# Cross terms of the second feed-forward product as seven block products in five of eight groups

## The chip, the cores and the metric

The kernel runs on one core of one Trainium2 chip. The metric is the device time of one execution in microseconds, as the median of several runs. Engines are named as the profile names them: PE is TensorE's matrix multiply, PEld its weight load, DVE is VectorE, ACT is ScalarE, POOL is GpSimd, SP is the engine that issues the DMAs.

## The reference, cut to what matters

x has 2048 tokens of D = 448 elements, F is 1792. One branch is a spectral filter over the whole array, the other a mixer whose last step is the feed-forward part that the change touches:

```python
xn = layernorm(x)
# spectral branch
A = irfft2(rfft2(xn) * (w_r + 1j * w_i), s=(S, D))
# mixer branch
h  = gelu(layernorm(xn) @ w1)
hs = concat(shift(h, +1, -1, +2, -2 on the four quarters)) @ w2
x1 = xn + hs
h2 = gelu(layernorm(x1) @ w3) @ w4
out = x + A + x1 + h2
```

The whole is computed close to float32 although TensorE is fed 16-bit numbers.

## The kernel before

**Halves.** Every float32 operand of a product is split into a high and a low float16 half, and a product is three: high by high, high by low and low by high. The last two are the cross terms.

**Tiles.** The 2048 tokens are 16 blocks of 128; block b holds tokens b, b + 16 and so on. The feed-forward part runs over eight groups G of two blocks (256 tokens) and, in each, over seven passes fp, each of which takes two of the fourteen 128-row slices of F. `front(G, fp)` (line 745) makes the 256 x 256 hidden values transposed: 22 matmuls of 256 columns at line 427 into one PSUM bank, whose tag ("mm", "tr") the caller gives. ACT then applies the gelu in place (line 753) and scales and copies the high half to `h` (line 756), and DVE subtracts to get the low half (line 757). `back(G, fp)` (line 761) multiplies by w4: for each of the two blocks, two slices by three products, twelve matmuls of 448 columns at line 776, added up over the seven passes in two PSUM banks of tag "acc". For the last block the columns are cut in two halves of 224 in two banks, so group 7 has 18 matmuls a pass: six of 448 and twelve of 224. After pass 6 DVE scales the sum and adds it to the block's tile (line 788, or line 783 with the store for groups 6 and 7, whose blocks wait in `rest`).

**Order.** `mlp` (line 791) issues fronts ahead of backs: two ahead in groups 0 to 2, with fronts over the tags mm and tr (four banks), one ahead in groups 3 to 7, with mm alone (two banks). It is called for group 0, groups 1 and 2, groups 3 to 5, group 6 and group 7; a call does not run ahead into the next. The tile framework orders each engine's queue by a planner with priorities: evacuations (EVAC) come first, the feed-forward matmuls (FILL) come last and fill what the spectral branch leaves. `behind(key)` makes what follows not issue before an earlier instruction: the folds and step1 are spread over passes by FOLD and PACE, the inverse by `units`. Each engine then runs its queue in order.

**What runs beside it.** Before group 0: layernorms, w1, shifts, w2. In group 0, w4 is split into halves, two slices at a time (`w4_split`, line 841, ACT and DVE), hooked behind the fronts. In groups 0 to 2 the spectral branch folds x (`do_fold`, line 562: load of two blocks, ACT, then four adds on POOL), splits it (`step1_in`, lines 584 and 585) and multiplies (`step1`, line 594, bank tag "sp"). During groups 3 and 4 sixteen chunks go through `chunk_a`, `chunk_b`, `chunk_z`, `chunk_c` (pp in a "tr" bank, px and pu in "sp" banks). From group 4, pass 4, to the end of group 6 each pass carries one inverse block: DVE gathers U (line 709), `inv_a` multiplies (pe, line 717, bank tag "tr"), ACT copies (line 721), POOL adds and subtracts (lines 724 and 725), DVE does four more (lines 726 to 729), ACT and DVE split into vh (lines 731 and 732), and `inv_b` multiplies (py, line 739, bank tag "sp") and DVE adds it to the block (line 740). `finish` (line 554) adds the input again (line 551) and stores.

**Memory.** PSUM has four tags of two banks each: mm, tr, acc, sp. `x2mem` (line 222) holds first w4 as loaded, then the transposed layernorm output of all groups. `wsrc` feeds warm-up matmuls at the start.

## Time and profile before

| what | value |
|---|---|
| three runs | 413.22, 412.57, 413.07 us, median 413.07 |
| profiled execution, first to last instruction (span) | 409.9 us |
| granted TensorE clock, mean | 1.000 |
| busy DVE, ACT, POOL over the span | 294.8, 247.8, 116.8 us |
| instructions | 8512 |

The profile is one execution; it gives its span, and no time of its own beside that. The runs are some 3 us longer than the span, since they hold what lies before the first and behind the last instruction.

A group row gives the line, engine, operation, tiles written and read, shapes, the count, then the busy time in us, the mean of one in ns, and the idle time of the engine just before with what ended it. A matmul's duration overlaps the next one's, so 352 ns of a 448-column matmul is not what it costs: the chain of work in order of time shows the spacing.

### The profile page before, as it was taken

The numbers are of one execution on the slowest core, as the hardware profiler recorded it, in microseconds if no ns is written. First come the engines' busy times: TensorE is split into PE (matmuls) and PEld (weight loads), VectorE is DVE, ScalarE is ACT, GpSimd is POOL, SyncE is SP. The second block draws the span as 40 slices with busy tenths as digits, with TensorE's granted clock in tenths as the row PEclk, the third lists the DMA queues.
The fourth block names the chain that finished last, engine by engine and source line by source line (L and its number), as shares of the span: only waits on it lengthen the run. The fifth ranks groups of instructions, "written<-read, shape, count | busy, mean of one in ns | idle before, by whom it ended". The sixth has DMA issues, their size and how long they took to land.

```text
span 409.9 us, 8512 instructions
## 1 busy us (share of the span) xinstructions
PE 404.8 (99%) x3295; PEld 288.1 (70%) x3295; DVE 294.8 (72%) x642; ACT 247.8 (60%) x427; POOL 116.8 (29%) x206
## 2 busy tenths in 40 slices
PE   8999999999999999999999999999999999999996
PEld 4554556666677877776887887877776777677885
DVE  5989999898644658863689889875777787667122
ACT  4689994884738756861688888873343434342321
POOL 3889820002308745400021221111222221121000
PEclk9999999999999999999999999999999999999999
DMA  8999999907712283527056555610000213223001
GB/s 278 335 269 200 172 178 248 269 2 183 137 43 56 79 300 106 143 63 164 14 162 167 145 147 142 182 43 2 2 0 2 73 55 100 91 76 128 24 0 46
DMA packets 57208, 49.45 MB, mean 121 GB/s; under 512 B 41312, under 2 KB 52192, under 8 KB 57168
## 3 DMA queue, kind: packets, MB, share of 16 engines
q1 hardware_dynamic: 57168, 48.91, 45.5%
q8 instruction: 26, 0.43, 0.4%
q14 instruction: 14, 0.11, 0.1%
HBM read 35.06 MB, written 3.67 MB: 95 GB/s over the span
## 4 chain that ended last, share of the span: by engine, by line
PE 96%; DMA 1%; POOL 1%; DVE 1%; issue 0%; POOLq 0%
PE pw L427 33%; PE acc L776 31%; PE pw L501 9%; PE pw L456 6%; PE pu L697 3%; PE ps L594 3%; PE pp L651 2%; PE pe L717 2%; PE px L668 2%; PE py L739 2%; PE wps L812 2%; DMA h<-hs 1%; PE pta L406 1%; POOL w2s L273 0%; POOL w2s L901 0%
## 5 line engine op out<-in xcount | busy, mean ns | idle before, releaser
L427 PE MATMUL pw<-x2mem,w3p 128*128 128x256 f16 x1232 | 149.1, 272 | 0.0
L776 PE MATMUL acc<-w4p,hf 128*128 128x448 f16 (+1 forms) x714 | 138.0, 341 | 0.0
L427 PEld LDWEIGHTS <-w3p 128*128 128x128 f16 x1232 | 118.6, 98 | 19.0
L776 PEld LDWEIGHTS <-hf 128*128 128x128 f16 x714 | 69.4, 98 | 48.3 <-DVE hf L757 0.3
L753 ACT ACTIVATE pw<-pw,pe 128x512 f32<-128x512 f32 x56 | 36.7, 655 | 63.1 <-PE pw L427 62.0
L757 DVE SCALAR_TENSOR_TENSOR hf<-pw,h,hf 128x512 f16<-128x512 f32 x56 | 42.0, 749 | 44.7 <-ACT hf L756 44.3
L756 ACT ACTIVATE hf<-pw,h 128x512 f16<-128x512 f32 x56 | 38.3, 684 | 1.2
L501 PE MATMUL pw<-w2p,h 112*128 112x448 f16 x192 | 38.8, 352 | 0.1
L678 POOL TENSOR_TENSOR z<-te 128x450 f32<-128x450 f32 x16 | 16.0, 1001 | 72.9 <-DVE te L676 69.1
L456 PE MATMUL pw<-w1p,xT 128*128 128x448 f16 x176 | 34.9, 352 | 0.5 <-DVE h L875 0.5
L724 POOL TENSOR_TENSOR e<-e 128x226 f32<-128x226 f32 x16 | 11.5, 720 | 77.8 <-ACT e L721 74.6
L501 PEld LDWEIGHTS <-h 112*128 112x128 f16 x192 | 18.5, 98 | 16.9 <-DMA h<-hs 0.9
L456 PEld LDWEIGHTS <-xT 128*128 128x128 f16 x176 | 17.0, 98 | 16.4 <-ACT xT L416 0.7
L658 ACT ACTIVATE pf<-pp 64x450 f16<-64x450 f32 x32 | 17.3, 541 | 16.7 <-DVE pf L659 8.3
L721 ACT ACTIVATE e<-pe 128x452 f32<-128x452 f32 x16 | 8.8, 547 | 26.4 <-PE pe L717 26.4
L659 DVE TENSOR_TENSOR pf<-pp,pf 64x450 f16<-64x450 f32 x32 | 19.9, 621 | 5.8 <-ACT pf L658 5.6
L574 POOL TENSOR_TENSOR xr<-xf 128x452 f32<-128x452 f32 x8 | 8.9, 1109 | 35.9 <-issue 27.1
L673 ACT ACTIVATE te<-px 64x450 f32<-64x450 f32 x32 | 17.2, 537 | 0.5
L585 DVE TENSOR_TENSOR xh<-f,xh 128x452 f16<-128x452 f32 x16 | 13.4, 878 | 5.3 <-ACT xh L584 5.3
L732 DVE TENSOR_TENSOR vh<-e,vh 128x448 f16<-128x448 f32 x16 | 10.0, 624 | 9.7 <-ACT vh L731 9.7
L577 POOL TENSOR_TENSOR f<-xr 128x452 f32<-128x452 f32 x16 | 16.4, 1045 | 0.6
L726 DVE TENSOR_TENSOR e<-e 128x113 f32<-128x113 f32 x16 | 9.9, 619 | 7.8 <-POOL e L724 7.8
(171 smaller groups left out, 598.8 us busy)
## 6 DMA issues: line engine op xcount, KB each, us to landing
wc<-wf SPq DMA_DIRECT2D x32, 225.0 KB, 3.5
wl<-wf SPq DMA_DIRECT2D x8, 450.0 KB, 4.1
xf<-x SPq DMA_DIRECT2D x8, 448.0 KB, 3.5
xt<-x SPq DMA_DIRECT2D x3, 896.0 KB, 12.1
w3raw<-w SPq DMA_DIRECT2D x3, 896.0 KB, 15.3
xr<-x SPq DMA_DIRECT2D x12, 224.0 KB, 2.6
out<-xr SPq DMA_DIRECT2D x12, 224.0 KB, 2.0
gn<-c_g SPq DMA_DIRECT2D x16, 128.0 KB, 3.2
```

Of the source, the lines that this page charges most:

```text
L427: T.matmul(ps_out, wp[:, wi + t, cols], xT[:, xi + t, tok], start=t == 0 and wi + xi == 0, stop=t == 3 and wi == 4)
L456: m = T.matmul(pm[:, :D], xTs[g][:, xi + t, 128 * i:128 * i + 128], w1p[:, wi + t], start=t == 0 and p == 0, stop=t == 3 and p == 2)
L501: m = T.matmul(w2b[b][:, :D], hT[g][:112, 4 * hi + k, o:o + 128], w2p[:, wi, k], start=k == 2 and hi + wi == 0, stop=k == 3 and hi == 1)
L577: P.tensor_tensor(out=f[:, :, k:k + 2].rearrange("p b s d -> p s b d"), in0=u[:, :, 0], in1=u[:, :, 1], op=op)
L658: A.activation(out=hi, in_=src, func=AF.Copy)
L659: V.tensor_tensor(out=lo, in0=src, in1=hi, op=ALU.subtract)
L673: i = A.activation(out=e[64 * h:64 * h + 64], in_=px_[64 - 64 * h:128 - 64 * h, :2 * DF], func=AF.Copy)
L678: P.tensor_tensor(out=z, in0=t[:, 0], in1=t[:, 1], op=ALU.add)
L753: A.activation(out=pm, in_=pm, func=AF.Gelu_apprx_tanh, scale=r3)
L756: i = A.activation(out=h[:, 0], in_=pm, func=AF.Copy, scale=h3)
L757: j = V.scalar_tensor_tensor(out=h[:, 1], in0=pm, scalar=h3, in1=h[:, 0], op0=ALU.mult, op1=ALU.subtract)
L776: m = T.matmul(to, h[:, hi, o:o + 128], w4p[0][:, wi, f, r], start=f == 0 and n == 0, stop=f == 13 and n == 2)
```

## The change

In groups 1, 2, 5, 6 and 7 (`STR`), but for passes 5 and 6 of group 7, the cross terms are no longer made block by block. A pass's two blocks of tokens, two slices of F and two halves of the columns form a 2 x 2 by 2 x 2 product of blocks of 128 x 128 by 128 x 224. For each cross term it is made by Strassen's scheme in Winograd's form: seven block products in place of eight. That needs

- four combinations of the blocks of `h`, for both halves (DVE, three instructions, in `front`);
- four combinations of the blocks of w4, for both halves (POOL, six instructions a pass, `w4_forms`, made once in group 0 and kept in `w4x` and `w4all`);
- fourteen matmuls of 224 columns a pass, three of the seven products straight into the group's `acc` banks and four into two banks of tag "tr" (`back`);
- at the end of the products of a group, two ACT copies out of these banks, four adds that combine them and two that add them to the blocks, on POOL, in group 7 on DVE.

The high-by-high matmuls stay. Groups 0, 3 and 4 keep their form. Besides, the fronts of groups 0 to 2 have the tag mm alone; pe and the two small products of `w_scale_end` go from tr to sp; in the inverse, `inv_b` of one block is issued after `inv_a` of the next; two waits in group 4 are behind earlier chunks; the scales of h and w4 are halved; the output of group 6 is stored after its adds; group 7's last block has its column halves only in passes 5 and 6, in tr banks. To make room, xT lies in `w4x`, `wsrc`, one of two `pf` buffers and the new `cross` buffer in `x2mem`, z in `xr`, and the fold's result takes the place of its input, with two buffers in place of three and two.

```diff
+STR = (1, 2, 5, 6, 7)
...
-    wsrc = pc.tile([128, 512], F16, name="wsrc")
+    x2mem = pw.tile([128, 9 * F], F16, name="x2mem")
+    wsrc = x2mem[:, 8 * F:8 * F + 512]
...
-    x2mem = pw.tile([128, 9 * F], F16, name="x2mem")
+    cross = x2mem.bitcast(F32)[:, 4 * F:4 * F + 2 * D].rearrange("p (i n) -> p i n", i=2)
     x2all = x2mem[:, 0:8 * F].rearrange("p (j t n) -> p j t n", j=4, t=7)
+    w4x = pw.tile([128, 48 * 224], F16, name="w4x")
...
+    def xT_of(g):
+        return w4x[:, 3584 * (g % 2):3584 * (g % 2) + 3584].rearrange("p (t n) -> p t n", t=7)
...
-        X = pfd.tile([128, 2, D + 1], F32, tag="xf", bufs=3, name=f"xf{b0}")
+        f = pfd.tile([128, 2, 4, 113], F32, tag="xf", bufs=2, name=f"xf{b0}")
+        X = f.rearrange("p b s d -> p (b s d)")[:, 0:2 * D + 2].rearrange("p (b d) -> p b d", b=2)
         after["X", b0] = (SY.dma_start(X[:, :, 0:D], xv[:, b0:b0 + 2]).ins,)
...
-        f = pfd.tile([128, 2, 4, 113], F32, tag="f", bufs=2, name=f"f{b0}")
...
-        pt = bank("tr", "wpt")
+        pt = bank("sp", "wpt")
...
-        pf = pst.tile([128, 2, 2, DF], F16, tag="pf", bufs=2, name=f"pf{c}")
+        pf = pf_buf[c % 2]
...
-        z = pst.tile([128, 2 * DF], F32, tag="z", bufs=2, name=f"z{c}")
+        z = xr[:, 2 * DF * (c % 2):2 * DF * (c % 2) + 2 * DF]
...
-        pe = bank("tr", f"pe{b}")
+        pe = bank("sp", f"pe{b}")
...
+    def crossed(G, fp):
+        return G in STR and (G, fp) not in ((7, 5), (7, 6))
...
-            with behind("te", 12) if (G, fp) == (4, 1) else contextlib.nullcontext():
+            with behind("te", 9) if (G, fp) == (4, 1) else contextlib.nullcontext():
                 A.activation(out=pm, in_=pm, func=AF.Gelu_apprx_tanh, scale=r3)
-            h = pw.tile([128, 2, 512], F16, tag="hf", bufs=3, name=f"hf{G}{fp}")
-            with behind("te", 10 + 2 * fp) if (G, fp) in ((4, 1), (4, 2)) else contextlib.nullcontext():
-                i = A.activation(out=h[:, 0], in_=pm, func=AF.Copy, scale=h3)
-                j = V.scalar_tensor_tensor(out=h[:, 1], in0=pm, scalar=h3, in1=h[:, 0], op0=ALU.mult, op1=ALU.subtract)
+            h = pw.tile([128, 2, 8, 128], F16, tag="hf", bufs=3, name=f"hf{G}{fp}")
+            pv_ = pm.rearrange("p (s n) -> p s n", s=4)
+            with behind("te", 9 + fp) if (G, fp) in ((4, 1), (4, 2)) else contextlib.nullcontext():
+                i = A.activation(out=h[:, 0, 0:4], in_=pv_, func=AF.Copy, scale=h3)
+                j = V.scalar_tensor_tensor(out=h[:, 1, 0:4], in0=pv_, scalar=h3, in1=h[:, 0, 0:4],
+                                           op0=ALU.mult, op1=ALU.subtract)
+                if crossed(G, fp):
+                    V.tensor_tensor(out=h[:, :, 4], in0=h[:, :, 0], in1=h[:, :, 1], op=ALU.subtract)
+                    V.tensor_tensor(out=h[:, :, 5:7], in0=h[:, :, 2:3].to_broadcast([128, 2, 2, 128]), in1=h[:, :, 0:5:4],
+                                    op=ALU.subtract)
+                    V.tensor_tensor(out=h[:, :, 7], in0=h[:, :, 3], in1=h[:, :, 6], op=ALU.subtract)
             after["f", G, fp] = i.ins, j.ins
         hs[G, fp] = h
     def back(G, fp):
         h = hs.pop((G, fp))
+        n = D // 2
+        end = 4 if G == 7 else 6
         if fp == 0:
             acc[G] = [bank("acc", f"acc{G}{i}") for i in range(2)]
-            if G == 7:
-                acc[G].append(bank("sp", "acc72"))
+            if G in STR:
+                xs[G] = [bank("tr", f"cr{G}{i}") for i in range(2)]
+        if (G, fp) == (7, 5):
+            xs[G] = [bank("tr", f"end{i}") for i in range(2)]
+        C = [[(slice(0, D), acc[G][i][:, 0:D], 0, 6)] for i in range(2)]
+        if G == 7:
+            C[1] = [(slice(0, D), acc[G][1][:, 0:D], 0, 4)]
+            if fp > 4:
+                C[1] = [(slice(n * k, n * k + n), xs[G][k][:, 0:n], 5, 6) for k in range(2)]
         for i in range(2):
-            b = 2 * G + i
-            c = D // 2 if b == NB - 1 else D
-            parts = [(slice(o, o + c), acc[G][i + o // c][:, 0:c]) for o in range(0, D, c)]
-            for r, to in parts:
+            for r, to, s, e in C[i]:
                 with behind("m", G, fp) if (G, fp) == (7, 6) and ("m", G, fp) in after else contextlib.nullcontext():
-                    for f in (2 * fp, 2 * fp + 1):
-                        for n, (hi, wi) in enumerate(((0, 0), (0, 1), (1, 0))):
-                            o = 256 * (f % 2) + 128 * i
-                            m = T.matmul(to, h[:, hi, o:o + 128], w4p[0][:, wi, f, r],
-                                         start=f == 0 and n == 0, stop=f == 13 and n == 2)
+                    for f in range(2):
+                        for hi, wi in ((0, 0),) if crossed(G, fp) else ((0, 0), (0, 1), (1, 0)):
+                            m = T.matmul(to, h[:, hi, 2 * f + i], w4p[0][:, wi, 2 * fp + f, r],
+                                         start=fp == s and f == 0 and hi + wi == 0, stop=fp == e and f == 1 and hi == 1)
                 after["m", G, fp] = (m.ins,)
-            if fp == 6 and b in rest:
-                t = rest.pop(b)
-                with prio(EVAC):
-                    for r, to in parts:
-                        V.scalar_tensor_tensor(out=t[:, r], in0=to, scalar=p34[:, 1:2], in1=t[:, r],
-                                               op0=ALU.mult, op1=ALU.add)
-                        SY.dma_start(ov[:, b, r], t[:, r])
-            elif fp == 6:
-                with prio(EVAC):
-                    V.scalar_tensor_tensor(out=xb(b), in0=acc[G][i][:, :D], scalar=p34[:, 0:1], in1=xb(b),
-                                           op0=ALU.mult, op1=ALU.add)
+        if crossed(G, fp):
+            X = [xs[G][k // 2][:, n * (k % 2):n * (k % 2) + n] for k in range(4)]
+            H = [[acc[G][i][:, n * k:n * k + n] for k in range(2)] for i in range(2)]
+            forms = [(0, 1, X[0], 9), (1, 3, H[1][0], 9), (3, 2, H[0][0], C[0][0][3]), (6, 4, X[2], 9),
+                     (4, 5, X[3], end), (5, 6, X[1], end), (2, 7, H[1][1], C[1][0][3])]
+            for hi, wi in ((0, 1), (1, 0)):
+                for k, slot, to, e in forms:
+                    m = T.matmul(to, h[:, hi, slot], w4f[fp][k][wi], start=k in (0, 6) and fp == 0 and hi == 0,
+                                 stop=hi == 1 and fp == e)
+            after["m", G, fp] = (m.ins,)
...
+        k34 = p34[:, 1:2] if G >= 6 else p34[:, 0:1]
+        to = {i: rest[2 * G + i] if G >= 6 else xb(2 * G + i) for i in range(2)} if fp >= 4 else {}
+
+        def evacuate(i):
+            for r, src, _, e in C[i]:
+                if fp == e:
+                    V.scalar_tensor_tensor(out=to[i][:, r], in0=src, scalar=k34, in1=to[i][:, r], op0=ALU.mult, op1=ALU.add)
+                    if G == 7 and fp == 6:
+                        SY.dma_start(ov[:, 2 * G + i, r], to[i][:, r])
+
+        with prio(EVAC):
+            if G in STR and fp == end:
+                e0, e1 = cross[:, 0], cross[:, 1]
+                for i in range(2):
+                    A.activation(out=cross[:, i], in_=xs[G][i][:, 0:D], func=AF.Copy, scale=k34)
+                for o, x, y in ((e0[:, n:], e0[:, 0:n], e0[:, n:]), (e1[:, 0:n], e1[:, 0:n], e0[:, n:]),
+                                (e0[:, n:], e0[:, n:], e1[:, n:]), (e1[:, n:], e1[:, 0:n], e1[:, n:])):
+                    (V if G == 7 else P).tensor_tensor(out=o, in0=x, in1=y, op=ALU.add)
+            for i in range(2):
+                evacuate(i)
+                if G in STR and fp == end:
+                    (V if G == 7 else P).tensor_tensor(out=to[i], in0=to[i], in1=cross[:, 1 - i], op=ALU.add)
+                if G == 6 and fp == 6:
+                    SY.dma_start(ov[:, 2 * G + i], to[i])
 
...
+    def w4_forms(fp):
+        n, f = D // 2, 2 * fp
+        b = [[w4p[0][:, :, f + r, n * c:n * c + n] for c in range(2)] for r in range(2)]
+        m = w4all[:, 56 * 224:] if fp == 6 else w4x[:, 8 * 224 * fp:8 * 224 * (fp + 1)]
+        m = m.rearrange("p (k n) -> p k n", n=224)
+        t1 = [m[:, 6], m[:, 7]]
+        t2, t3, t4 = (m[:, k:k + 4:3] for k in range(3))
+        P.tensor_tensor(out=t3, in0=b[1][1], in1=b[0][1], op=ALU.add)
+        for i in range(2):
+            P.tensor_tensor(out=t1[i], in0=b[0][0][:, i], in1=b[0][1][:, i], op=ALU.subtract)
+            P.tensor_tensor(out=t2[:, i], in0=b[1][1][:, i], in1=t1[i], op=ALU.subtract)
+        P.tensor_tensor(out=t4, in0=b[1][0], in1=t2, op=ALU.subtract)
+        w4f[fp] = [[x[:, i] for i in range(2)] for x in (b[0][0], b[1][0], b[1][1], t4)]
+        w4f[fp] += [t1] + [[x[:, i] for i in range(2)] for x in (t2, t3)]
...
-    V.tensor_scalar(out=h3, in0=s3, scalar1=2.0 ** -5, scalar2=None, op0=ALU.mult)
+    V.tensor_scalar(out=h3, in0=s3, scalar1=2.0 ** -6, scalar2=None, op0=ALU.mult)
...
-    s4, r4 = powers(m4, 7, "4")
+    s4, r4 = powers(m4, 7, "4", down=1)
...
-    w4p[0] = pa.tile([128, 2, 14, D], F16, tag="R", bufs=1, name="w4p")
+    w4all = pa.tile([128, 64 * 224], F16, tag="R", bufs=1, name="w4p")
+    w4p[0] = w4all[:, 0:56 * 224].rearrange("p (i f n) -> p i f n", i=2, f=14)
...
-    mlp([0], hook=w4_rest, ahead=AH, tags=("mm", "tr"))
+                w4_forms(fp)
+        else:
+            with behind("f", G, fp):
+                w4_forms(fp)
+
+    mlp([0], hook=w4_rest, ahead=AH, tags=("mm",))
...
-    mlp([1, 2], ahead=AH, tags=("mm", "tr"))
+    mlp([1, 2], ahead=AH, tags=("mm",))
...
+    pf_buf = [pst.tile([128, 2, 2, DF], F16, name="pf0"),
+              x2mem[:, 8 * F:8 * F + 4 * DF].rearrange("p (a b n) -> p a b n", a=2, b=2)]
...
     def inverse(ns):
         for n in ns:
-            gather_u(bs[n])
-            with behind("m", *units[n]):
-                inv_a(bs[n])
-            with behind("m", *units[min(n + LAG, 20 - INV)]):
-                inv_b(bs[n])
-            if bs[n] < 12:
-                finish(bs[n])
+            if n < 16:
+                gather_u(bs[n])
+                with behind("m", *units[n]):
+                    inv_a(bs[n])
+            if n:
+                with behind("m", *units[min(n - 1 + LAG, 20 - INV)]):
+                    inv_b(bs[n - 1])
+                if bs[n - 1] < 12:
+                    finish(bs[n - 1])
     inverse(range(4))
     mlp([6], last=True)
-    inverse(range(4, 16))
+    inverse(range(4, 17))
     mlp([7], last=True)
...
-    nc = bacc.Bacc("TRN2", target_bir_lowering=False, num_devices=1)
+    nc = bacc.Bacc("TRN2", target_bir_lowering=False, num_devices=1, dynamic_dma_scratch_size=512)
```

More of the change, by code (lines that the diff above doesn't have):

```diff
@@ L431, in body @@
     w3p = pa.tile([128, 8, F], F16, name="w3p")
-    w4p = {}
+    w4p, w4f = {}, {}
     w1p = p1.tile([128, 8, D], F16, name="w1p")
```

16 lines of the change are left out of this document (8 added, 8 removed).

## The prediction

> **What bounds the kernel now.** I read first the totals by engine and the chain of work that ended last, both on the page.
>
> ```profile
> span 409.9 us, 8512 instructions
> ...
> PE 404.8 (99%) x3295; PEld 288.1 (70%) x3295; DVE 294.8 (72%) x642; ACT 247.8 (60%) x427; POOL 116.8 (29%) x206
> ...
> PE 96%; DMA 1%; POOL 1%; DVE 1%; issue 0%; POOLq 0%
> PE pw L427 33%; PE acc L776 31%; PE pw L501 9%; PE pw L456 6%; PE pu L697 3%; PE ps L594 3%; PE pp L651 2%; PE pe L717 2%; PE px L668 2%; PE py L739 2%; PE wps L812 2%; DMA h<-hs 1%; PE pta L406 1%; POOL w2s L273 0%; POOL w2s L901 0%
> ```
>
> TensorE is the end of the chain for 96% of the span, and the line to be changed, L776, holds 31% of it. A page can call a pipelined engine busy while it waits, so I next took the chain in order of time, where each piece is so many matmuls and the stretch they set.
>
> ```profile
> 117.93 1.34 PE ps L594 x24
> ...
> 358.72 2.41 PE pw L427 x22
> 361.13 2.27 PE acc L776 x12
> ...
> 378.64 2.29 PE acc L776 x18
> ...
> 402.08 4.58 PE acc L776 x36
> ```
>
> These are the real spacings. Twelve matmuls of 448 columns take 2.27 us: 0.189 us each. In group 7 a pass has 18: six of 448 (6 x 0.189 = 1.135) and twelve of 224, so (2.29 - 1.135) / 12 = 0.0962 us each. The time follows the columns, plus very little. L594's 128-column matmuls come every 1.34 / 24 = 0.056 us, each with its own weight load, so loads do not hold up a 224-column one. Last, the busy time of the engines by stretch (columns: stretch, its length, then PE, weight loads, DVE, ACT, POOL).
>
> ```profile
> 95.00:118.00 23.00, 23.00 (x163) 15.47 (x161) 14.01 (x37) 13.26 (x21) 5.86 (x7) 1.00 0.67 151
> 118.00:161.70 43.70, 43.70 (x399) 33.82 (x397) 27.10 (x34) 30.77 (x56) 26.04 (x24) 1.00 0.39 128
> 161.70:194.00 32.30, 32.30 (x272) 23.33 (x271) 20.77 (x34) 18.48 (x31) 4.77 (x7) 1.00 0.48 117
> ...
> 293.00:332.00 39.00, 39.00 (x326) 27.76 (x325) 28.75 (x68) 14.29 (x25) 9.91 (x14) 1.00 0.08 25
> 332.00:372.90 40.90, 40.90 (x344) 29.42 (x342) 30.23 (x67) 16.21 (x28) 8.78 (x14) 1.00 0.26 85
> 372.90:406.70 33.80, 33.74 (x285) 27.43 (x282) 10.56 (x19) 10.02 (x15) 0.00 (x0) 1.00 0.11 35
> ```
>
> They are groups 0, 1, 2, then 5, 6 and 7. TensorE is full in all of them at clock 1.00, so column time taken out of L776 comes off the end, if nothing else becomes late. DVE is what could: 59.0 of 79.9 us in groups 5 and 6.
>
> **What the change removes on TensorE.** A changed pass keeps its four high-by-high matmuls of 448 columns and replaces eight cross matmuls of 448 by fourteen of 224 (seven products, high by low and low by high). 8 x 0.189 = 1.514 us become 14 x 0.0962 = 1.347: 0.167 us less. Groups 1, 2, 5, 6 have 28 such passes: 4.67 us. In group 7, passes 0 to 4 go from 2.29 us to 4 x 0.189 + 1.347 = 2.10: 0.186 x 5 = 0.93. Passes 5 and 6 there keep their forms, so the last 4.58 us of the chain and the store stay. Together 5.60 us, the ceiling.
>
> The Trainium skill (TensorE: Matmul & The Clock Gate, Back-to-back issue gap) says that a stream of weight load and matmul pairs sustains 81 ns at 128 columns and 131 ns at 512. A straight line through those would be an estimate of 94 ns at 224 columns and 123 at 448, and by it fourteen halves cost 0.33 us more than eight wholes. The chain pieces disagree: 56, 96 and 189 ns.
>
> **What it adds elsewhere.** The costs come from the groups of instructions with shapes kept apart (busy us, mean ns of one, idle before), and from one DVE line taken in group 1 and then in group 2.
>
> ```profile
> L776 PEld LDWEIGHTS <-hf 128*128 128x128 f16 x714 | 69.4, 98 | 48.3 <-DVE hf L757 0.3
> L757 DVE SCALAR_TENSOR_TENSOR hf<-pw,h,hf 128x512 f16<-128x512 f32 x56 | 42.0, 749 | 44.7 <-ACT hf L756 44.3
> L756 ACT ACTIVATE hf<-pw,h 128x512 f16<-128x512 f32 x56 | 38.3, 684 | 1.2
> L753 ACT ACTIVATE pw<-pw,pe 128x512 f32<-128x512 f32 x56 | 36.7, 655 | 63.1 <-PE pw L427 62.0 <-DVE U L709 1.2
> ...
> L577 POOL TENSOR_TENSOR f<-xr 128x452 f32<-128x452 f32 x16 | 16.4, 1045 | 0.6
> ...
> L725 POOL TENSOR_TENSOR e<-e 128x226 f32<-128x226 f32 x16 | 10.1, 628 | 0.0
> L732 DVE TENSOR_TENSOR vh<-e,vh 128x448 f16<-128x448 f32 x16 | 10.0, 624 | 9.7 <-ACT vh L731 9.7
> ...
> L721 ACT ACTIVATE e<-pe 128x452 f32<-128x452 f32 x16 | 8.8, 547 | 26.4 <-PE pe L717 26.4
> ...
> L709 DVE COPY U<-y 113x512 f16<-113x512 f16 x32 | 8.0, 300 | 2.8 <-PE pe L717 2.8
> ...
> L728 DVE TENSOR_TENSOR e<-e 128x112 f32<-128x112 f32 x16 | 4.2, 264 | 0.0
> ```
>
> ```profile
> L585 DVE TENSOR_TENSOR xh<-f,xh 128x452 f16<-128x452 f32 x10 | 9.9, 1031 | 4.1 <-ACT xh L584 4.1
> ```
>
> ```profile
> L585 DVE TENSOR_TENSOR xh<-f,xh 128x452 f16<-128x452 f32 x4 | 2.3, 620 | 0.0
> ```
>
> *DVE, three combinations of h a pass* (256, 512 and 256 elements, 16-bit). No row has two 16-bit tensors. Not below 0.26 (L728) + 0.30 (L709's 16-bit copy) + 0.26 = 0.82 us; not above f32 prices, 0.42 (between L728 and L732) + 0.75 (L757) + 0.42 = 1.59. I take 1.0: the 16-bit copy is the nearest kind, with something for the second operand. In groups 5 and 6 that is 14 us against 79.9 - 59.0 = 20.9 idle. Queued behind them on DVE stand the inverse's butterflies and the scaling of py, for which pe and py on TensorE wait; what DVE waits for now in those groups (293 to 372.9 us) is this, as total, times, longest:
>
> ```profile
> DVE vh L732 <- ACT vh L731: 9.7, 11, 1.1
> DVE e L726 <- POOL e L724: 6.2, 12, 0.8
> DVE xt L740 <- PE py L739: 3.3, 10, 0.3
> ```
>
> Of 19.2 us of waits three quarters must be filled by the new work, or inverse blocks slide into group 7, where DVE has 23 us free. I charge 0.4 us; from nothing up to the second rival.
>
> *The lock in group 1.* L585 takes 1.03 us while POOL is at work 26.0 of 43.7 us and 0.62 where it is at work 4.8 of 32.3: an op that reads two SBUF tensors waits about 0.41 us. The 21 new ones of group 1 read two: 27.1 + 7.0 + 8.6 = 42.7 us of DVE in 43.7 - 1.2 = 42.5. Full, but crosses are issued two passes after their front, so lateness is absorbed into group 2 (20.8 + 7.0 of 31.1). Charge 0.4; up to 4.3 (first rival). The Trainium skill (SBUF — State Buffer, SBUF: two separate sides) has the mechanism: one port pair, held for a whole instruction by GpSimd or by a DVE op with two SBUF inputs. These rows agree.
>
> *POOL, the w4 forms.*
>
> ```profile
> 90.45 2.21 DVE L288 SCALAR_TENSOR_TENSOR w4p<-x2mem,pe,w4p 128x896 f16<-128x896 f32 x2
> ```
>
> ```profile
> 195.23 0.71 PE pp L651 x12
> ```
>
> Per pass two adds of 448 and four of 224, 2 x 1.05 + 4 x 0.63 = 4.6 us, 32 in all, from the first two splits of w4 on, which end at 92.7 us. Their cover is group 0, 5.9 of 23 us in use, and group 1, which takes one form set per pass. Behind them on POOL are the folds; 5.9 + 26.0 + 32.2 + 4.6 = 68.7 us from 92.7 to 161.7 just fits, and step1 (L594), which waits for the folds, has until the chunks, whose first product (pp) comes at 195. Without that cover each late fold would hold a step1 of TensorE; with it TensorE runs products meanwhile. Charge 0.
>
> *End of a group*: two ACT copies (0.55 each) free the cross banks 1.3 us after the last product, while the next front (2.41) and four direct matmuls run. Six adds, 4.6 us of POOL (DVE in group 7, idle there), delay group 6's two stores, 30 us ahead of the end. No DMA is added; x for the folds has two buffers for three, but loads of pairs two apart are due three passes apart. Charge 0; if a bank came late, about 1 us a group.
>
> *Two banks for the fronts of groups 0 to 2, and h at group starts.*
>
> ```profile
> 115.06 0.49 PE L427 MATMUL pw<-x2mem,w3p 128*128 128x256 f16 x3
> ...
> 116.14 0.27 PE L427 MATMUL pw<-x2mem,w3p 128*128 128x256 f16 x1
> ...
> 119.10 6.93 PE L427 MATMUL pw<-x2mem,w3p 128*128 128x256 f16 x62
> ```
>
> ```profile
> 121.27 0.66 ACT L753 ACTIVATE pw<-pw,pe 128x512 f32<-128x512 f32 x1 [1.37 <-PE pw L427]
> 121.96 0.69 ACT L756 ACTIVATE hf<-pw,h 128x512 f16<-128x512 f32 x1
> ...
> 122.68 0.75 DVE L757 SCALAR_TENSOR_TENSOR hf<-pw,h,hf 128x512 f16<-128x512 f32 x1 [2.06 <-ACT hf L756]
> ```
>
> ```profile
> 333.04 4.59 PE pw L427 x42
> 337.63 2.36 PE acc L776 x12
> ```
>
> Front (1,0) has 4 of its 22 matmuls done before 119.10, ends at 119.10 + 18 x 0.109 = 121.07, and its bank is free at 123.43, 2.36 us later. The third front would take that bank one front (2.40) later: just in time. In steady order a pass and more lies between. Charge 0.3, up to 1. At the start of group 6 the first front ends at 333.04 + 20 x 0.109 = 335.22 and its pass begins 2.41 us later. The direct matmuls need only ACT's copy; the products come 0.757 later, at 3.16, and need 2.36 + 1.0 = 3.36. So 0.2 us at the starts of groups 6 and 7: 0.4, from 0 to 1.6.
>
> **Sum.** -5.60 + 0.4 + 0.4 + 0.3 + 0.4 = -4.1 us: the span 409.9 becomes 405.8. The three runs have a median of 413.07 (412.57 to 413.22); the 3.2 us outside the span stay. Forecast 409.0 us, its own range 407.7 to 410.4.
>
> **Rivals.** *The lock takes groups 1 and 2's share.* At the f32 price group 1's DVE has 27.1 + 11.1 + 8.6 = 46.8 us for 42.5: 4.3 late, so 413.07 - 5.60 + 1.1 + 4.3 = 412.9; halfway 411. For it: L585's 1.03. Against: POOL is nearly idle in group 2. Time 412.
>
> *DVE becomes the bound in groups 5 and 6*, the other side. A pass there now has 79.9 / 14 = 5.71 us with 59.0 / 14 = 4.21 of DVE. With 1.59 added and half of the 19.2 / 14 = 1.37 us of waits left open, 4.21 + 1.59 + 0.69 = 6.49: 0.78 more a pass, 10.9 in all. The other groups give 0.93 + 28/2 x 0.167 = 3.3, less 1.1: 413.07 + 10.9 - 2.2 = 421.8. It costs time from 5.54 us a pass on and makes the kernel slower above 5.71 + 2.2 / 14 = 5.87, that is when additions and open waits exceed 1.66. Against it: short ops can stand in the waits for ACT, and group 7's idle DVE.
>
> *Nothing is late*: 413.07 - 5.60 = 407.5. Today TensorE hides every DVE wait.
>
> *The halves do not do what the count says.* A load row of L776 lasts 98 ns, longer than the 96 of a half. Were a product's load not hidden under the matmul before it, the spacing would be 0.0962 + 0.098 = 0.194 and a pass would take 14 x 0.194 - 1.514 = 1.2 us more, 39.7 over 33 passes: 452. It turns against the change from 1.514 / 14 = 0.108 us on. Group 7's twelve halves at 0.0962, loads included, speak against it. The Trainium skill's line above (TensorE: Matmul & The Clock Gate, Back-to-back issue gap) would give, as an estimate, 33 x 0.33 = 10.9 us more, about 424.
>
> **How the numbers follow.** Forecast 0.52, nothing late 0.13, lock 0.15, DVE bound 0.18, slow halves 0.02. A difference under 0.2% (0.8 us) cannot be told from none. Faster: 0.52 + 0.13 + 0.09 of the lock = 0.74; same 0.06, the rest of the lock; slower 0.18 + 0.02 = 0.20. The range runs from just under "nothing late", 407.0, to 413.9, beyond the lock at its upper price; it leaves out the slower cases, 0.20.
>
> **What would show it.** Right: fourteen products in 1.35 us, TensorE full in groups 5 to 7, group 7's product passes at 4.5 us from 4.69. Wrong: product weight loads or matmuls that wait for h on DVE inside groups 5 or 6 (second rival), DVE full in group 1 with new ops over 0.7 us (first), fronts of groups 0 to 2 that wait for L757, or step1 waiting for POOL. If products come at 0.1 us or more, the ceiling itself was wrong.

## The result, and the profile after

| | median us | range | ratio to before on the same chip |
|---|---|---|---|
| before (4 runs) | 412.82 | 411.84 to 413.22 | |
| after (4 runs) | 426.56 | 424.79 to 428.44 | 1.0349, 95% interval 1.0312 to 1.0386 |

The change makes the kernel 13.7 us slower. The profiled run took 426.34 us with a span of 424.6. Totals and chain of the page after:

```profile
span 424.6 us, 9061 instructions
...
PE 404.3 (95%) x3463; PEld 305.2 (72%) x3463; DVE 351.0 (83%) x748; ACT 254.0 (60%) x437; POOL 175.0 (41%) x272
...
PE 60%; DVE 19%; ACT 6%; POOL 5%; DMA 5%; issue 4%; ACTq 0%; POOLq 0%; SPq 0%
```

TensorE held 96% of the chain before; now DVE has 19% of it. TensorE is busy 404.3 us against 404.8, so fewer columns did not become less busy time; and it is idle 424.6 - 404.3 = 20.3 us against 409.9 - 404.8 = 5.1. What it was idle for is in the view of waits (TensorE line, who ended the wait: us, times, longest), first before, then after:

```profile
PE wps L812 <- DVE wsrc L186: 1.2, 1, 1.2
PE pw L456 <- DVE h L875: 0.5, 1, 0.5
```

```profile
PE pw L433 <- DVE hf L767: 7.3, 1, 7.3
PE ps L600 <- DVE y L605: 2.9, 2, 2.4
PE wps L856 <- DVE x2mem L188: 1.2, 1, 1.2
PE acc L807 <- DVE hf L773: 1.0, 1, 1.0
PE ps L600 <- ACT y L604: 1.0, 1, 1.0
...
PE cr L807 <- DVE hf L771: 0.7, 1, 0.7
...
PE ps L600 <- DVE xh L591: 0.5, 1, 0.5
PE pw L462 <- DVE h L934: 0.5, 1, 0.5
```

The 1.2 us at the start and the 0.5 before L462 were there before. New are one wait of 7.3 us, in which a front (L433) has no bank because DVE's low half of h (L767) is late; 4.4 us in which step 1 (L600) waits; and four short ones of 1.0 us or less. The stretches (columns as in the prediction), before and then after, place the long wait in group 0:

```profile
90.00:112.00 22.00, 22.00 (x155) 15.00 (x154) 16.37 (x42) 14.29 (x23) 4.69 (x10) 1.00 0.68 147
```

```profile
90.00:112.00 22.00, 14.22 (x94) 8.98 (x92) 21.76 (x34) 10.38 (x16) 22.00 (x31) 0.94 0.47 104
112.00:131.00 19.00, 18.60 (x119) 12.53 (x119) 10.91 (x15) 5.44 (x10) 17.63 (x21) 0.89 0.13 26
...
162.00:208.00 46.00, 42.64 (x413) 36.41 (x411) 39.54 (x72) 28.98 (x52) 18.84 (x20) 0.96 0.64 172
307.80:348.20 40.40, 40.40 (x404) 33.83 (x401) 38.87 (x105) 17.71 (x31) 12.94 (x18) 1.00 0.08 25
348.20:390.70 42.50, 41.51 (x400) 34.50 (x398) 38.30 (x90) 17.76 (x32) 14.73 (x20) 1.00 0.26 82
```

The last two rows are groups 5 and 6. From 90 to 112 us POOL works without a gap, almost all of it on the combinations of w4, and DVE is busy 21.76 of 22 us, yet has run fewer instructions (34 for 42). The same stretch by DVE line (busy us, mean ns), before and after; L288 became L291, L542 L548, L301 L304, L757 L767, L508 L514:

```profile
L288 DVE SCALAR_TENSOR_TENSOR w4p<-x2mem,pe,w4p 128x896 f16<-128x896 f32 x5 | 5.6, 1144 | 0.0
L757 DVE SCALAR_TENSOR_TENSOR hf<-pw,h,hf 128x512 f16<-128x512 f32 x4 | 3.0, 749 | 0.1
L542 DVE SCALAR_TENSOR_TENSOR y<-y,vs 128x384 f16<-128x384 f32 x4 | 2.4, 611 | 0.0
L508 DVE SCALAR_TENSOR_TENSOR xt<-xt,cs,pw 128x448 f32<-128x448 f32 x3 | 2.0, 671 | 0.0
...
L301 DVE SCALAR_TENSOR_TENSOR nqb<-nqb 128x4 f32<-128x4 f32 x2 | 0.3, 148 | 0.0
```

```profile
L291 DVE SCALAR_TENSOR_TENSOR w4p<-x2mem,pe,w4p 128x896 f16<-128x896 f32 x4 | 6.1, 1553 | 0.0
L548 DVE SCALAR_TENSOR_TENSOR y<-y,vs 128x384 f16<-128x384 f32 x2 | 2.0, 1004 | 0.0
L514 DVE SCALAR_TENSOR_TENSOR xt<-xt,cs,pw 128x448 f32<-128x448 f32 x3 | 2.0, 669 | 0.0
...
L304 DVE SCALAR_TENSOR_TENSOR nqb<-nqb 128x4 f32<-128x4 f32 x2 | 1.6, 792 | 0.0
...
L767 DVE SCALAR_TENSOR_TENSOR hf<-pw,h,hf 128x512 f16<-128x512 f32 x2 | 1.5, 737 | 0.0
```

L291, L548 and L304 read two operands from SBUF (a row names a tile once, though L304 reads it twice). They are longer, by about 0.4 us the large ones and 0.6 the one of four elements a partition, which grew fivefold. L514 and L767, one of whose two operands lies in PSUM, are as before; but L767 ran twice where it ran four times, since it stands in DVE's queue behind the others. The lengthening is a wait inside the instruction. The timeline (start, duration), DVE first, then POOL:

```profile
106.92 0.96 DVE L302 TENSOR_TENSOR nqb<-nib 128x4 f32<-128x4 f32 x1
...
109.52 0.56 DVE L304 SCALAR_TENSOR_TENSOR nqb<-nqb 128x4 f32<-128x4 f32 x1
110.12 0.95 DVE L305 SCALAR_TENSOR_TENSOR nwb<-nqb,nib 128x4 f32<-128x4 f32 x1
```

```profile
106.83 1.03 POOL L895 TENSOR_TENSOR w4x<-w4p 128x448 f16<-128x448 f16 x1
...
109.16 0.91 POOL L898 TENSOR_TENSOR w4x<-w4p,w4x 128x224 f16<-128x224 f16 x1
110.03 1.03 POOL L899 TENSOR_TENSOR w4x<-w4p,w4x 128x448 f16<-128x448 f16 x1
```

The three DVE operations end at 107.88, 110.08 and 111.07 us; POOL's end at 107.86, 110.07 and 111.06. Each of these small DVE operations ends with POOL's. The Trainium skill (SBUF — State Buffer, Who interferes with whom) says that a DVE operation with two SBUF inputs and a GpSimd instruction that reads SBUF contend, that one in a two-port mode contends with GpSimd too, that whoever issues first holds the shared ports for its whole instruction, and that a DVE operation with at most one SBUF input outside those modes does not contend. The rows of L291, L548 and L304 and those of L514 and L767 agree.

The chain in order of time shows what follows the wait:

```profile
111.61 0.75 DVE hf L767
112.40 4.41 PE pw L433 x22
...
188.11 4.03 PE pw L433 x22
...
398.73 0.76 PE acc L797 x4
400.83 2.40 PE pw L433 x22
403.23 0.76 PE acc L797 x4
```

After the long wait, and after the step-1 waits ahead of 188 us, 22 matmuls of a front take 4.4 and 4.0 us instead of 2.40, while the granted clock of these stretches is 0.94, 0.89 and 0.96. The Trainium skill (TensorE: Matmul & The Clock Gate, Part 1) has TensorE fall to half its clock after an idle window of about 3.4 us; the 7.3 us fit. The waits ahead of 188 us, 2.4 and 1.0 us with 0.8 us of matmuls between them, are each shorter, so why the clock fell there is not shown. In group 7 the products do what was reckoned: a pass takes 403.23 - 398.73 = 4.50 us.

### The profile page after: what moved, and what is told of

It is laid out like the page before. It is cut to its first block, busy times and chain, and to the rows that moved or that the text cites. A ratio compares the mean times of both kernels' runs of the same rounds, so it can differ in the third digit from the quotient of the medians.

```text
span 424.6 us, 9061 instructions
## 1 busy us (share of the span) xinstructions
PE 404.3 (95%) x3463; PEld 305.2 (72%) x3463; DVE 351.0 (83%) x748; ACT 254.0 (60%) x437; POOL 175.0 (41%) x272
## 4 chain that ended last, share of the span: by engine, by line
PE 60%; DVE 19%; ACT 6%; POOL 5%; DMA 5%; issue 4%; ACTq 0%; POOLq 0%; SPq 0%
PE pw L433 20%; PE acc L797 13%; PE pw L462 4%; PE pw L507 3%; PE cr L807 3%; PE acc L807 3%; PE pu L703 2%; PE px L674 2%; DMA xf<-x 2%; PE pp L657 2%; PE wps L856 2%; DVE hf L767 2%; DVE xr L557 2%; POOL x2mem L827 1%; DVE w4p L291 1%
## 5 line engine op out<-in xcount | busy, mean ns | idle before, releaser
L433 PE MATMUL pw<-x2mem,w3p 128*128 128x256 f16 x1232 | 155.0, 276 | 7.3 <-DVE hf L767 7.3
L433 PEld LDWEIGHTS <-w3p 128*128 128x128 f16 x1232 | 120.7, 99 | 27.2 <-issue 7.6
L797 PE MATMUL acc<-w4p,hf 128*128 128x448 f16 x396 | 85.8, 352 | 0.6 <-ACT hf L766 0.6
L797 PEld LDWEIGHTS <-hf 128*128 128x128 f16 x420 | 40.6, 98 | 26.8 <-ACT hf L766 0.9
L767 DVE SCALAR_TENSOR_TENSOR hf<-pw,h,hf 128x512 f16<-128x512 f32 x56 | 41.7, 745 | 20.4 <-ACT hf L766 20.2
L807 PEld LDWEIGHTS <-hf 128*128 128x128 f16 x462 | 44.0, 98 | 9.2 <-DVE hf L773 1.5
L684 POOL TENSOR_TENSOR xr<-te 128x450 f32<-128x450 f32 x16 | 15.7, 983 | 66.0 <-DVE te L682 62.3
L507 PE MATMUL pw<-w2p,h 112*128 112x448 f16 x192 | 39.0, 352 | 0.9 <-DVE xt L514 0.8
L462 PE MATMUL pw<-w1p,w4x 128*128 128x448 f16 x176 | 34.9, 352 | 0.5 <-DVE h L934 0.5
L807 PE MATMUL acc<-w4p,hf 128*128 128x224 f16 x140 | 30.4, 259 | 1.0 <-DVE hf L773 1.0
L507 PEld LDWEIGHTS <-h 112*128 112x128 f16 x192 | 18.4, 98 | 18.0 <-issue 1.0
L462 PEld LDWEIGHTS <-w4x 128*128 128x128 f16 x176 | 17.0, 98 | 16.5 <-ACT w4x L422 0.7
L807 PE MATMUL cr<-w4x,hf 128*128 128x224 f16 x174 | 27.4, 259 | 0.7 <-DVE hf L771 0.7
L827 POOL TENSOR_TENSOR x2mem<-x2mem 128x224 f32<-128x224 f32 x16 | 11.6, 723 | 28.7 <-ACT x2mem L824 27.8
L771 DVE TENSOR_TENSOR hf<-hf 128x512 f16<-128x512 f16 x33 | 20.1, 611 | 0.7
L807 PE MATMUL cr<-w4p,hf 128*128 128x224 f16 x90 | 20.5, 259 | 0.0
L583 POOL TENSOR_TENSOR xf<-xr 128x452 f32<-128x452 f32 x16 | 17.4, 1107 | 0.5
```

Of the source, the lines that this page charges most:

```text
L433: T.matmul(ps_out, wp[:, wi + t, cols], xT[:, xi + t, tok], start=t == 0 and wi + xi == 0, stop=t == 3 and wi == 4)
L462: m = T.matmul(pm[:, :D], xTs[g][:, xi + t, 128 * i:128 * i + 128], w1p[:, wi + t], start=t == 0 and p == 0, stop=t == 3 and p == 2)
L507: m = T.matmul(w2b[b][:, :D], hT[g][:112, 4 * hi + k, o:o + 128], w2p[:, wi, k], start=k == 2 and hi + wi == 0, stop=k == 3 and hi == 1)
L583: P.tensor_tensor(out=f[:, :, k:k + 2].rearrange("p b s d -> p s b d"), in0=u[:, :, 0], in1=u[:, :, 1], op=op)
L767: j = V.scalar_tensor_tensor(out=h[:, 1, 0:4], in0=pv_, scalar=h3, in1=h[:, 0, 0:4], op0=ALU.mult, op1=ALU.subtract)
L771: V.tensor_tensor(out=h[:, :, 5:7], in0=h[:, :, 2:3].to_broadcast([128, 2, 2, 128]), in1=h[:, :, 0:5:4], op=ALU.subtract)
```

## The experiments

Each kernel is the changed one but for its edit; times are medians, ratios those to the kernel before on the same chip with their 95% interval. The experiments ran on several chips, so the difference of two of them is taken from their ratios (0.01 is 4.1 us). Step-1 waits in the expectations (6.4 us and the like) count all time beyond the usual spacing of the matmuls; the waits' rows hold 4.7 us of those 6.4.

**The combinations of w4 left out (e1).**

```diff
-        m = w4all[:, 56 * 224:] if fp == 6 else w4x[:, 8 * 224 * fp:8 * 224 * (fp + 1)]
...
-        w4f[fp] += [t1] + [[x[:, i] for i in range(2)] for x in (t2, t3)]
+        pick = (b[0][0], b[1][0], b[1][1], b[0][1], b[0][0], b[1][0], b[1][1])
+        w4f[fp] = [[x[:, i] for i in range(2)] for x in pick]
```

> Left out: the combinations of w4 are not made; the products take w4's own blocks in their place, so matmuls and DVE work are as in the changed kernel. Theory L (POOL's w4 additions hold back DVE's operations with two SBUF inputs in group 0, so that a front waits for its bank): the 10.4 us that TensorE loses between 90 and 112 us go, 413 to 417 us. Rival B (two banks for the fronts are too few by themselves): 424 to 427. Rival D (the products' own additions make DVE late): 423 to 427, with the losses in groups 1, 2, 5 and 6.

416.18 us, 1.0108 (1.002 to 1.0196, two runs). The page and the first waits:

```profile
PE 399.5 (97%) x3463; PEld 303.3 (73%) x3463; DVE 337.6 (82%) x748; ACT 253.7 (61%) x437; POOL 139.7 (34%) x230
```

```profile
PE ps L600 <- DVE y L605: 3.0, 2, 2.6
...
PE ps L600 <- ACT y L604: 1.0, 1, 1.0
PE ps L600 <- DVE xh L591: 0.7, 1, 0.7
```

The wait for L767 is down to 0.6 us and two thirds of the loss are gone. The same 3463 matmuls keep TensorE busy 399.5 us instead of 404.3: the 4.8 us between are the half clock. Against the 404.8 of before, the products save 5.3 us. POOL has 175.0 - 139.7 = 35 us less. The largest wait that remains is step 1's.

**The reverse: combinations made, no products (e4).** `STR = ()`.

> No group uses the products (STR is empty); the combinations of w4 are still made on POOL, and banks and buffers are those of the changed kernel. L: the 10 us of group 0 stay: 421 to 426 us. D: the time falls back to 413 to 416. B and L together differ from D here only by group 0; what lies above 413 beside group 0 is the price of banks and buffers.

423.47 us, 1.0285 (1.0255 to 1.0315).

```profile
PE pw L433 <- DVE hf L767: 7.4, 1, 7.4
```

The long wait is there without a single product and without one combination of h. The 11.9 us are the price of the combinations of w4 together with that of the changed kernel's banks and buffers.

**The banks of group 0's fronts (e2).** `tags=("mm",)` for group 0 becomes `tags=("mm", "tr")`.

> Fronts of group 0 over four banks again (tags mm and tr), nothing else changed. B: the wait of 7.4 us for the bank and the half clock behind it go, 415 to 418 us. L: DVE is as late as before, so the wait moves from the front's bank to h or the split of w4, and the time falls by less: 419 to 425. D: no change, 425 to 428.

426.91 us, 1.0369 (1.0333 to 1.0404): no better. TensorE now waits for the same DVE instruction one step later, 5.2 us at L797. As DVE is held here too, the run does not tell what two banks cost by themselves; e10 below does.

**The same additions on DVE (e7).** In `w4_forms`, `P.tensor_tensor` becomes `V.tensor_tensor`.

> The combinations of w4 on DVE in place of POOL, all else as changed. By the durations of the three combinations of h without a wait (0.28, 0.41, 0.28 us) a pass costs about 2 us of DVE, 14 in all, in groups 0 and 1. L: no wait for POOL, the small operations stay at 0.15 us, 416 to 421 us. If the amount of DVE work and not the lock makes group 0 late: 423 us and more.

416.94 us, 1.0116 (1.0075 to 1.0157), by the ratios 0.3 us above e1, which makes none, and well inside both intervals. The stretch of group 0 and its L767:

```profile
90.00:112.00 22.00, 21.78 (x153) 14.80 (x152) 21.54 (x66) 13.07 (x22) 5.43 (x8) 1.00 0.57 123
```

```profile
L767 DVE SCALAR_TENSOR_TENSOR hf<-pw,h,hf 128x512 f16<-128x512 f32 x4 | 3.0, 756 | 0.5 <-ACT hf L766 0.5
```

DVE is as full as in the changed kernel (21.54 of 22 us), but with 66 instructions instead of 34, and L767 comes four times again. It was not the amount of work for DVE but POOL's instructions beside it.

**POOL at work, without reading (e6).** The six additions of a pass become six memsets of the same area.

> In place of the six additions of a pass POOL writes zeros six times into the same memory (896 elements each), at the same places of the program; the products take w4's own blocks. POOL is kept busy but reads nothing. Theory L (DVE is held back by POOL operations that read SBUF): as e1_forms_out, 414 to 418 us, and DVE's 4-element operations in group 0 at 0.15 us. Rival Q (what stands behind the additions in POOL's queue comes late): 419 to 426, by as much as the writes keep POOL busy.

425.81 us, 1.0331 (1.0291 to 1.0371). The memsets wait for nothing and ran ahead of group 0, so the time tests neither theory there. The loss lies ahead of group 0, and the trace shows which DVE operations a memset holds. Timeline, DVE first, then POOL:

```profile
61.64 2.18 DVE L291 SCALAR_TENSOR_TENSOR w3p<-w3raw,pe,w3p 128x896 f16<-128x896 f32 x2
...
72.40 6.14 DVE L299 TENSOR_SCALAR nib<-vb 128x2 int32<-128x2 int32 x1
```

```profile
61.64 1.62 POOL L893 MEMSET w4x<- 128x896 f16 x2
...
71.39 0.84 POOL L893 MEMSET w4p<- 128x896 f16 x1
...
77.68 0.84 POOL L893 MEMSET w4p<- 128x896 f16 x1
```

Two instructions of L291, with two SBUF operands, take 2.18 us beside the memsets and 2.17 at the same place of the changed kernel, where none run: a memset, which reads nothing, does not hold them as the additions do. L299, a TENSOR_SCALAR on int32 with one SBUF input, is held, from 72.40 us to the end of the last memset of a gapless series at 78.5, where it takes 0.16 us in the kernel before; three operations behind it on DVE end together with it. TensorE then waits 2.6 us at L507 for DVE. (At 11 us another TENSOR_SCALAR, L272, takes 2.47 us for 0.45, and TensorE waits 2.5 us at L462.) So theory L is right about the operations with two SBUF inputs, and wrong that a POOL instruction that reads nothing cannot make DVE late.

**Combinations meant for group 3 (e8).** Products in groups 5 to 7 only, four banks for the fronts of groups 0 to 2 as before, and `w4_forms` called behind the fronts of group 3.

> Products in groups 5, 6 and 7 alone, the combinations of w4 made on POOL behind the fronts of group 3, fronts of groups 0 to 2 over four banks. L: groups 0 to 2 run as before the change; in group 3 the additions hold back two of some seven DVE operations of a chunk, which TensorE covers with fronts and backs: 410.5 to 414 us. If the chunks are late beyond what the fill covers: 415 to 420. The ceiling would be 413 - 3.3 = 409.8.

420.48 us, 1.0202 (1.0172 to 1.0231).

```profile
PE acc L797 <- DVE hf L767: 4.6, 1, 4.6
```

The edit did not move them: `behind` orders instructions of one engine, and a front's records are ACT's and DVE's, so POOL still ran the additions in group 0. The run counts as the price of the combinations in group 0, with the products of groups 1 and 2 and the fronts' two banks out of the way: beside e10 below, which makes none and has the same products and banks, 8.1 us.

**The same, held back by an instruction of POOL (e9).**

```diff
-STR = (1, 2, 5, 6, 7)
+STR = (5, 6, 7)
...
-        P.tensor_tensor(out=z, in0=t[:, 0], in1=t[:, 1], op=ALU.add)
+        after["z", c] = (P.tensor_tensor(out=z, in0=t[:, 0], in1=t[:, 1], op=ALU.add).ins,)
...
-    mlp([0], hook=w4_rest, ahead=AH, tags=("mm",))
+    mlp([0], hook=w4_rest, ahead=AH, tags=("mm", "tr"))
...
-    mlp([1, 2], ahead=AH, tags=("mm",))
+    mlp([1, 2], ahead=AH, tags=("mm", "tr"))
...
+    for fp in range(7):
+        with behind("z", 2 * fp + 1):
+            w4_forms(fp)
```

> Products in groups 5 to 7 only, the kernel before's banks in groups 0 to 2, and the combinations of w4 still on POOL but each pass of them queued behind POOL's addition of an odd chunk of the transform (L684), so that they run beside groups 3 and 4 and none in group 0. Theory 'POOL holds DVE' (the price of the combinations is what POOL's instructions do to DVE in group 0, where DVE has no room): the 4 to 5 us wait for hf L767 in group 0 is gone, L304 to L307 on 128x4 fall to about 0.15 us there; 411.5 to 416 us, by how much room DVE has in groups 3 and 4. Rival 'the combinations cost the same wherever they stand' : 419 to 422 us, as with them in group 0 (420.5 us), the wait appearing in groups 3 and 4 instead.

413.09 us, 1.0039 (1.0024 to 1.0054), by the ratios 6.7 us less than e8 for the same work in another place. In group 0 L767 runs four times from 90 to 112 us and TensorE is busy all 22. Where the additions went, 199 to 252 us, with the DVE lines of 199 to 292 us; first here, then in the next but one, e10, which makes none:

```profile
199.00:252.00 53.00, 52.02 (x565) 43.19 (x563) 49.81 (x76) 43.89 (x81) 40.14 (x45) 1.00 0.60 151
...
L682 DVE SCALAR_TENSOR_TENSOR te<-te,sc,wc 128x450 f32<-128x450 f32 x16 | 12.6, 790 | 0.0
...
L680 DVE SCALAR_TENSOR_TENSOR te<-px,sc,wc 128x450 f32<-128x450 f32 x16 | 10.9, 681 | 1.8 <-ACT te L679 1.5
```

```profile
199.00:252.00 53.00, 52.52 (x571) 43.64 (x569) 48.32 (x79) 45.60 (x84) 12.29 (x12) 1.00 0.64 159
...
L680 DVE SCALAR_TENSOR_TENSOR te<-px,sc,wc 128x450 f32<-128x450 f32 x16 | 10.9, 684 | 3.6 <-ACT te L679 3.5
...
L682 DVE SCALAR_TENSOR_TENSOR te<-te,sc,wc 128x450 f32<-128x450 f32 x16 | 10.8, 677 | 0.0
```

28 us more of POOL cost TensorE 0.5 us there (and the whole kernel 1.4 us by the ratios of e9 and e10, the rest of which was not traced), although DVE is busy over nine tenths of the time in both. Most of DVE's work in these groups reads PSUM, like L680, and is not held; L682, with two operands in SBUF, grows by 0.11 us.

**Groups 5 to 7 with the combinations on DVE (e11), and with none (e10).** Both with the edits of `STR` and `tags` of e9; e11 with e7's edit, e10 with e1's.

> As the changed kernel, but products in groups 5 to 7 only, the banks of the kernel before in groups 0 to 2, and the combinations of w4 on DVE instead of POOL. Theory 'POOL holds DVE': group 0 loses at most 1.5 us although DVE has all 38 instructions of additions more; 412 to 414.5 us. Rival 'DVE has no room in group 0, whoever takes it': the wait for hf L767 is as long as with POOL, 419 us or more.

> No combinations of w4 are made (the products take blocks of w4 itself, so the cross part of the output is not the reference's), products in groups 5 to 7 only, and the banks of the kernel before in groups 0 to 2. If the step-1 waits that stayed in groups 1 and 2 without products there (2.1 us at 166.9 to 175.8 us) come from the fronts' two banks: they go, and the time is 411 to 412 us. If they come from something else: unchanged at 413.7 us. Either way the 1.2 and 0.8 us at the ends of groups 5 and 6 stay, against a saving of some 3.4 us in TensorE time.

e11: 413.35 us, 1.0047 (1.0032 to 1.0062); L797 waits 1.4 us for L767 in group 0, as the theory allowed. e10: 411.83 us, 1.0005 (0.9993 to 1.0017). It differs from e5 below (1.0041, 1.0025 to 1.0058) only in the four banks of the fronts of groups 0 to 2: two banks cost about 1.5 us. From 90 to 112 us TensorE is busy 22.00 us here and 21.58 in e5, from 150 to 190 us 39.09 and 38.33, so the step-1 waits fell by about half and did not go. And even without the combinations the products of three groups gain nothing that can be told from none. By the prediction's terms they save 14 x 0.167 + 5 x 0.186 = 3.3 us; the page of e10 has TensorE busy 402.5 us of a span of 410.5, 2.3 less than before, and idle 8.0, 2.9 more, in short waits: 0.8 us at L600, 0.7 and 0.4 at L807, 0.5 at L674. No version here beats the kernel before.

**Step 1 in groups 1 and 2.** The first guess was the fold's two buffers for x; e3 gives it three and finds the room elsewhere.

```diff
-        f = pfd.tile([128, 2, 4, 113], F32, tag="xf", bufs=2, name=f"xf{b0}")
+        f = pfd.tile([128, 2, 4, 113], F32, tag="xf", bufs=3, name=f"xf{b0}")
```

> Three buffers for x of the folds in place of two (for the room, cross lies elsewhere in x2mem and one xh buffer in x2mem's tail). Theory F (loads of x wait for a buffer, so folds and step1 come late and TensorE loses 6.7 us in groups 1 and 2): 419 to 422 us, no ACT wait over 1 us for xf. If the folds are late because of POOL and DVE: 425 to 428, with step1 still waiting.

430.1 us, 1.0446 (1.0361 to 1.0531): the time that theory F gave did not come. The run is no clean test, though. ACT's wait for the loads of x falls from 4.4 us to 0.3 and step 1 waits 2.0 us instead of 4.4, but the fronts wait 10.5 us for DVE instead of 7.3 and the products 2.7 instead of 1.7. What part the buffers have stays open. Then e5, which is e1 with `STR = (5, 6, 7)`:

> As e1_forms_out (no combinations of w4, w4's own blocks in their place), and products in groups 5, 6 and 7 alone. In e1_forms_out TensorE still lost 6.4 us on step1 in groups 1 and 2. Theory P (the products' DVE additions, held back by the folds on POOL, make step1 late): those waits go and the 2.3 us that groups 1 and 2 gained go too, 411 to 413.5 us. Rival B2 (banks and buffers make step1 late): 416 to 419, with step1 still waiting.

413.69 us, 1.0041 (1.0025 to 1.0058): without products in groups 1 and 2, and with two buffers still, the waits of step 1 fall from 4.7 to 1.0 us. What of the products does it is told by e12 (e1 and, in groups 1 and 2, no combinations of h), e13 (e1 and, there, none of the six additions L827 and L831) and e14 (both):

```diff
-                if crossed(G, fp):
+                if crossed(G, fp) and G > 2:
...
-                    m = T.matmul(to, h[:, hi, slot], w4f[fp][k][wi], start=k in (0, 6) and fp == 0 and hi == 0,
+                    m = T.matmul(to, h[:, hi, slot if G > 2 else slot % 4], w4f[fp][k][wi], start=k in (0, 6) and fp == 0 and hi == 0,
```

```diff
-                    (V if G == 7 else P).tensor_tensor(out=o, in0=x, in1=y, op=ALU.add)
+                    if G > 2:
+                        (V if G == 7 else P).tensor_tensor(out=o, in0=x, in1=y, op=ALU.add)
...
-                if G in STR and fp == end:
+                if G in STR and fp == end and G > 2:
```

> No combinations of w4 are made, and in groups 1 and 2 none of h: the products take blocks of w4 and of h themselves there (the cross part of the output is not the reference's). All the rest is the changed kernel's. Theory P (in groups 1 and 2 DVE is full: the three combinations of h per pass, held by POOL's folds and cross additions, make the copies of step 1 late): the step-1 waits of groups 1 and 2 (6.4 us at 132.8 to 176.0 us with the combinations of h) fall to 1.5 us or less, 411 to 412.5 us. Rival (the additions of the cross terms on POOL, L827 and L831, in the folds' queue make step 1 late): the waits stay above 4 us, 415 to 417 us.

> No combinations of w4 are made (the products take w4's own blocks), and in groups 1 and 2 the six additions of the cross terms on POOL (L827, L831) are left out, so the cross part of those groups is not the reference's; the combinations of h stay there. Theory A (the additions, 5.7 us of POOL at two places in the folds' queue, make step 1 late): the step-1 waits of groups 1 and 2 fall from 6.4 us to under 3, 412 to 414 us. Theory P (DVE full by the combinations of h): they stay at 4 us or more, 415 to 416.5 us. If both carry a half: about 414.5 us.

> As e13, and in groups 1 and 2 no combinations of h either (the products take blocks of h itself). If combinations and additions together are what makes step 1 late, the waits there fall to the 1.2 us that also stay with products in groups 5 to 7 only, and the time is 411 to 412 us. If something else of the products does it (the cross banks that the fronts had before, the larger h), the waits stay near the 3.6 us left with the combinations of h alone taken out: 413.5 to 414.5 us.

| kernel | median us | ratio | waits at L600, us |
|---|---|---|---|
| e1 | 416.18 | 1.0108 (1.002 to 1.0196) | 4.7 |
| e12, no combinations of h | 414.37 | 1.0068 (1.0042 to 1.0094) | 2.9 |
| e13, no additions | 415.16 | 1.0082 (1.0052 to 1.0112) | 4.0 |
| e14, neither | 412.23 | 1.0019 (0.9994 to 1.0044) | 1.7 |

Neither theory alone holds: e12 missed the 1.5 us that theory P gave it, e13 the 3 of theory A. Each removal takes a part, by the ratios the combinations of h 1.6 or 2.6 us, the additions 1.1 or 2.0 (without or with the other removed), both together 3.7; the intervals of e1 and e13 are wide, so the split is rough, and the waits are those of one execution each, for e13 the slowest of its seven. Each removal takes away the work as well as what it holds up; the runs do not part the two. The 1.7 us left were not traced further.

## Why the prediction was wrong

*What adds up.* In the profiled runs, idle TensorE rose by 20.3 - 5.1 = 15.2 us, the half clock took 4.8, and the products saved 5.3: 14.7 us, the difference of the spans.

*The step that failed* is "POOL, the w4 forms", with its "Charge 0". Its 32 us were 35, near enough; its cover was wrong. It counted the free time of POOL ("5.9 of 23 us in use") and looked for what waits for POOL. No wait of TensorE names the forms. What suffered was DVE beside them. That operations with two SBUF operands wait for POOL stood just above, as 0.41 us from L585, under "The lock in group 1", but it was charged to the 21 new instructions there and not to the old ones of group 0, where POOL was to become full. Nor did group 1 take "one form set per pass": the additions ran from 87.8 to 131.1 us, and group 0 ends at about 129. The rows show the price: L291 grew by 0.41 us an instruction (1553 - 1144 ns), L548 by 0.39 and L304 by 0.64, which is 3.7 us over the eight that ran from 90 to 112 us, and about 10 with L300, L302, L303, L305, L306, L307, L539 and L546. By this L767 came late, and the front waited for it, in the prediction's words "fronts of groups 0 to 2 that wait for L757". The prediction names these waits among its signs of being wrong, but none of its rivals had the cause. The forms in group 0 cost 8.1 us by e8 and e10 and 9.9 by the changed kernel and e1, the latter roughly; e7 and e9 showed that it is POOL's work at that place.

*The half clock* was not reckoned with: a long wait costs TensorE again behind it, 4.8 us in all.

*TensorE's saving* was right: 5.3 us for 5.60, passes of group 7 at 4.50 as named. The slow-halves rival is out.

*DVE, three combinations of h.* 1.0 us a pass was right where nothing holds them (0.28, 0.41 and 0.28 in the trace of e10), and 1.41 as the mean of the changed kernel (0.346, 0.611 and 0.457).

*The lock in group 1*, 0.4 us, and *End of a group*, 0, were mis-sized: together 3.7 us (e1 to e14). The additions stand in POOL's queue ahead of the folds that step 1 waits for, and can hold DVE as well; which of the two counts more was not tested. The first rival had DVE in group 1 at 4.3 us; its near size is in part luck, since the additions on POOL, which it did not charge, carry 1.1 to 2.0 us.

*DVE as the bound in groups 5 and 6* did not come: DVE is busy 38.87 of 40.4 and 38.30 of 42.5 us there, but TensorE is idle for 0 and 0.99. That is one wait of the products for L773 at 372 us, against a charge of 0.4; the products' wait for h at the start of group 7 was 0.7, also against 0.4.

*Two banks for the fronts*, 0.3 us "up to 1", were 1.5 (e5 and e10).

*What lies outside the span*, 3.2 us, was taken from the median of the runs and the span of a profile; in the profiled run of the changed kernel, which has both, it is 1.7 us (426.34 - 424.6).

With the forms, and in groups 1 and 2 the combinations of h and the additions, left out, the kernel (e14) is still at 1.0019, where the prediction's ceiling was 5.60 us of gain. Its trace has TensorE idle for 9.9 us, 4.8 more than before, of which its rows name 4.4: 1.7 at step 1, 1.7 at L807, 0.6 at L797 for ACT, 0.4 for a front's bank. So with all of that removed the change would still be about even with the kernel before.

## What to carry to other kernels

An engine's free time is not free to fill: before work goes onto POOL, list what DVE runs in the same stretch with both operands in SBUF, and its TENSOR_SCALARs on SBUF, and add up to one POOL instruction's remaining time to each, small ones above all; then ask which queue position behind them TensorE waits for. If the work has to be on POOL, put it beside a stretch in which DVE reads PSUM, and hold it there with an instruction of POOL itself. A saving of 1.3% on the bound engine is small enough for a few waits of 1 us to eat it, and one long wait is paid twice where the clock falls behind it.

## What the runs showed of the hardware

DVE's L304 on four elements a partition took 0.148 us alone and 0.79 beside POOL's additions, while operations of 448 and 512 elements with an input in PSUM kept their 0.67 and 0.74 us. L300, a TENSOR_SCALAR on int32 with one input, was held too (0.57 us for 0.16). Beside memsets (e6) operations with two SBUF inputs were not held (L291 1.09 us each), but the like of L300 was: L299 waited 6.1 us, until a gapless series of memsets had ended, and not for one instruction only. POOL gained nothing from 16-bit operands: 1.03 us for 448 elements and 0.60 for 224 where nothing held it, as for float32 of the same size in the prediction's rows; in e7 DVE took 0.40 to 0.43 and 0.28 us for the same additions.
